# A three-stage attention and mixing kernel on one core: the order of TensorE's steps is written out, and the other engines' targets follow from it

## The chip, the core and the metric

The kernel runs on one core of one Trainium2 chip. The metric is the device time of one execution in microseconds (us). Before the change it is 635.29 us, the median of three runs (633.85 to 635.33). The execution that the profile recorded took 632.69 us.

## The reference

Three blocks follow each other for a batch of 4, 448 positions and a width of 768 (12 heads of 64):

```python
scores = np.where(mask, -1e9, scale * q @ k.T)
x = softmax(scores) @ v                       # 12 heads, joined to 768 columns
theta = x @ w_theta
y = w_tok_r @ (x * cos(theta)) + w_tok_i @ (x * sin(theta))
u = x + y
x = u + relu(u @ w_ch)
logits = x @ w_gate                           # top 2 of 4 experts, softmax over the two
for e in range(4):                            # each expert is causal attention with one head of 64
    out += weight[e] * (softmax(mask(x @ wq[e] @ (x @ wk[e]).T)) @ (x @ wv[e]) @ wo[e])
```

All of it is float32.

## The kernel before

The program doesn't emit its instructions as they are written. Each call of an engine (`pe`, `act`, `dve`, `pool`, `sp`) is recorded by `Plan.add` (L203) as a step with its dependencies, its tiles and a cost estimate, and `Plan.issue` (L327) then plays a clock forward over five engines and emits steps as they become ready. All real instructions are emitted from one line of a helper (L508 in the profile), so that the profile tells them apart by tile and not by line. On the chip each engine follows the order in which its instructions were emitted, and waits where a result or a buffer isn't there yet.

What orders the steps is a due time. `plan.due` is set by the code around a step from the numbers in `K` (L521): a start and a length for each stage. `rank` (L313) pulls the due times of producers ahead of their users. In `issue`, an engine takes the ready step with the earliest due time; for TensorE a step of another kind than the last one (`mode`, L197) gets `K["pen"]` added (L436), so that the kinds are not mixed without need. Some steps may go to one of several engines (`either`, L286): copies out of PSUM to ScalarE or VectorE, scalings to GpSimd or ScalarE, and so on; `issue` decides by who would be done first. Buffers of one tag (`unit` 6, `pa` 2, `ph` 2, `raw` 3, `zn` 3, the PSUM tags `tp` 6 and `mm` 2; L545 to L547) are handed out in the order in which the program's text asks for them (`turn`).

The stages, per batch b, as the list `ORDER` (L520) has them:

- `attn1` (a0 to a3, L771): six pairs of heads. A pair (`pair`, L644) has six score matmuls with 64 rows and one of 448 columns with 128 rows (tiles `tp<-raw`), softmax on VectorE and ScalarE into `pa`, scaling by GpSimd and ScalarE, then `pa` is transposed: either by 16 TensorE transposes (`tp<-ident,pa`) that are copied to `ph` by ScalarE or VectorE, or, for the pairs in `BYDVE`, on VectorE and by 16 DMAs `ph<-pa` from SyncE. 20 matmuls `tp<-ph,vt` end it.
- `mixing` (m0 to m3, L812): x is split into a high and a low part of the type fp32r (`hl`), since a matmul in fp32r is a single pass; three products each stand for one full product. Six theta products of 18 matmuls (`mm<-hl,unit`), sine and cosine into `zt`, transposes (`tp<-ident,zt`), copies and differences into `zn`, and six products of 21 matmuls (`mm<-wt,zn`).
- `project` (p0 to p3, L875): six products with w_ch and four for queries and keys (`mm<-zt,unit`, 18 matmuls each, the latter into `qp`), and the values and gate logits (`mm<-unit,zt`, 260 columns).
- `attn2` (c0 to c3, L980): two pairs as in `attn1` but from `qp`, and six products with wo (`tp<-hc,c`).

Weights are read once as float32, split on VectorE, ScalarE and GpSimd, and written to DRAM (`scr<-unit`); later batches load the split form (`unit<-scr`), two tiles for one product. All DMAs are issued by SyncE (SP), in one order. The kernel starts with 24 transposes of the identity (`mm<-ident`) before the first scores.

Of the kernel before, what the change touches and what calls it, by code (L numbers as in the profile page):

```python
# [23 lines left out]
P = 128  # L24
# [96 lines left out]
SWITCH = 200.0  # L121
MODE = SWITCH
# [4 lines left out]
class Step:  # L127
    __slots__ = ("calls", "soft", "heirs", "after", "options", "done", "engine", "cost", "due", "deps", "users", "waiting", "ready", "tiles", "fresh", "order", "lag", "pc", "lk", "issued", "at", "mode")


class Plan:
# [3 lines left out]
    def __init__(self, nc, tc):  # L135
        self.nc, self.tc = nc, tc
        self.steps = []
        self.due = 0.0
        self.after = 0.0
# [8 lines left out]
    def cost(self, engine, name, out, ins, kw):  # L148
        n = out.width if isinstance(out, View) else 0
        psum = any(v.root.psum for v in ins)  # L150
        if engine == "tensor":
# [5 lines left out]
            if self.mode(ins, name):  # L157
                return 8.0 + 0.86 * n
# [4 lines left out]
        if engine == "vector":  # L163
            if name == "tensor_tensor_reduce":
                n = ins[0].width
            if name == "tensor_reduce":
                n = ins[0].width
            if name == "transpose":
                return 66.0 + 1.13 * n
# [27 lines left out]
    def mode(ins, name):  # L197

        if name != "matmul" or ins[1].dtype != F32:
            return 0  # L200
        return 1 if ins[0].idx.shape[0] == 1 else 2 if ins[0].width == 64 else 0

    def add(self, engine, name, *args, **kw):  # L203
# [13 lines left out]
        else:  # L217
# [5 lines left out]
            step.due = self.due  # L223
            step.lag = 0.0
            step.mode = self.mode(ins, name) if engine == "tensor" else 0
            step.after = self.after
# [44 lines left out]

    def claim(self, view):
# [40 lines left out]
    def rank(self):  # L313
# [12 lines left out]

    def issue(self):  # L327
# [6 lines left out]
        self.rank()  # L334
# [56 lines left out]
        while count < len(self.steps):  # L391
# [13 lines left out]
            for e in order:  # L405
# [5 lines left out]
                for x in avail[e]:  # L411
# [4 lines left out]
                    if pick is not None and due >= best:  # L416
                        break
# [15 lines left out]
                    if e != "tensor":  # L433
                        pick = x
                        break
# [15 lines left out]
                if e == "tensor":  # L451
                    if now < COLD:
                        end += cost
                    if s.mode != mode:
                        end += SWITCH
# [55 lines left out]
class Engine:  # L511
# [3 lines left out]
    def __getattr__(self, method):  # L515
# [5 lines left out]
K = {"path": 0.9449731, "hop": 186.6965, "slack": 134.3007, "war": 624.4051, "ahold": 15406.4476,  # L521
# [9 lines left out]
     "warm": 24}  # L531
# [525 lines left out]
```

## Time and profile before

| | us |
|---|---|
| median of three runs | 635.29 |
| profiled execution | 632.69 |
| its span, from the first to the last instruction | 630.9 |
| TensorE busy with matmuls | 607.5 |
| VectorE busy | 424.1 |
| ScalarE busy | 327.0 |
| GpSimd busy | 119.8 |

The page first gives the busy time of each engine over the span. TensorE (PE) is the engine with the largest share, and its instructions are fixed in number, so that its idle time and its place in time are what to look at. Two queries tell those: the busy time by stretches of the span, and the waits of an engine, with what ended them. A stretch in which two engines are both nearly full needs a look at both.

### The profile page before, as it was taken

The numbers are of one execution on the slowest core, as the hardware profiler recorded it, in microseconds if no ns is written. First come the engines' busy times: TensorE is split into PE (matmuls) and PEld (weight loads), VectorE is DVE, ScalarE is ACT, GpSimd is POOL, SyncE is SP. The second block draws the span as 40 slices with busy tenths as digits, with TensorE's granted clock in tenths as the row PEclk, the third lists the DMA queues.
The fourth block names the chain that finished last, engine by engine and source line by source line (L and its number), as shares of the span: only waits on it lengthen the run. The fifth ranks groups of instructions, "written<-read, shape, count | busy, mean of one in ns | idle before, by whom it ended". The sixth has DMA issues, their size and how long they took to land.

```text
span 630.9 us, 12382 instructions
## 1 busy us (share of the span) xinstructions
PE 607.5 (96%) x4320; PEld 525.7 (83%) x4320; DVE 424.1 (67%) x1294; ACT 327.0 (52%) x869; POOL 119.8 (19%) x219
## 2 busy tenths in 40 slices
PE   7899989999998999999999999999999999999987
PEld 5686868789896999988878978988888999999876
DVE  4799999998847865347677688527756596515260
ACT  5999797553524643037767667126565251101473
POOL 3433356220112200004210213002110110000020
PEclk9899999999999999999999999999999999999999
DMA  9768541568749760685766771056753963157523
GB/s 332 273 218 284 171 173 29 162 218 297 245 130 277 232 229 2 196 244 146 243 187 208 267 255 31 1 147 196 226 150 112 314 183 102 32 181 238 161 62 122
DMA packets 54639, 114.76 MB, mean 182 GB/s; under 512 B 7601, under 2 KB 19377, under 8 KB 54577
## 3 DMA queue, kind: packets, MB, share of 16 engines
q1 hardware_dynamic: 54576, 113.98, 56.8%
q8 instruction: 34, 0.56, 0.4%
q14 instruction: 29, 0.23, 0.1%
HBM read 81.15 MB, written 21.26 MB: 162 GB/s over the span
## 4 chain that ended last, share of the span: by engine, by line
PE 70%; DVE 9%; DMA 3%; ACT 2%; SPq 1%; issue 1%; POOL 0%; DVEq 0%; ACTq 0%; POOLq 0%
PE mm L508 50%; PE tp L508 20%; DVE zt L508 3%; DMA unit<-scr 2%; DVE pa L508 2%; DVE cmb L508 2%; SPq L508 1%; ACT pa L508 1%; DVE st L508 1%; DVE tp L508 1%; DMA c<-scr 1%; DVE zn L508 1%; DMA vt<-v 0%; ACT L508 0%; POOL pa L508 0%
## 5 line engine op out<-in xcount | busy, mean ns | idle before, releaser
L508 PE MATMUL mm<-zt,unit 128*128 128x448 f32 x720 | 159.6, 373 | 0.6 <-ACT qp L508 0.6
L508 ACT ACTIVATE pa<-pa,st 128x128 f32<-128x128 f32 (+4 forms) x257 | 125.0, 516 | 44.5 <-DVE st L508 34.9
L508 PEld LDWEIGHTS mm<-zt,unit 128*128 128x128 f32 x720 | 133.9, 188 | 15.9 <-issue 4.0
L508 PE MATMUL mm<-wt,zn 128*128 128x448 f32 x504 | 117.3, 375 | 0.4 <-DVE st L508 0.4
L508 POOL TENSOR_SCALAR pa<-pa,st 128x384 f32<-128x384 f32 (+3 forms) x114 | 65.6, 588 | 222.7 <-DVE st L508 154.3
L508 PE MATMUL mm<-hl,unit 128*128 128x448 f32 x432 | 97.8, 376 | 3.9 <-DMA unit<-scr 2.0
L508 PEld LDWEIGHTS mm<-wt,zn 128*128 128x128 f32 x504 | 91.5, 188 | 9.6 <-issue 1.4
L508 PEld LDWEIGHTS mm<-hl,unit 128*128 128x128 f32 x432 | 79.7, 189 | 15.8 <-DVE zt L508 3.2
L508 DVE CUSTOM_DVE_ANT_0 pa<-tp,mask 128x384 f32<-128x384 f32 (+3 forms) x147 | 58.6, 444 | 10.6 <-PE tp L508 10.4
L508 PE MATMUL tp<-raw 64*128 64x384 f32 (+3 forms) x336 | 61.3, 425 | 0.0
L508 PE MATMUL tp<-ident,pa 128*128 128x128 f32 x336 | 45.3, 277 | 8.4 <-POOL pa L508 4.4
L508 ACT ACTIVATE pa<-tp,st 128x256 f32<-128x256 f32 (+3 forms) x77 | 37.7, 510 | 27.2 <-DVE st L508 27.1
L508 PEld LDWEIGHTS tp<-ident,pa 128*128 128x128 f32 x336 | 37.9, 141 | 15.9 <-POOL pa L508 7.4
L508 PEld LDWEIGHTS tp<-raw 64*128 64x128 f32 (+1 forms) x336 | 34.1, 190 | 16.9 <-issue 4.7
L508 ACT ACTIVATE ph<-tp 128x512 f32<-128x512 f32 x67 | 35.5, 593 | 22.5 <-PE tp L508 22.4
L508 PE MATMUL tp<-ph,vt 128*64 128x128 f32 (+1 forms) x960 | 46.6, 254 | 0.0
L508 PEld LDWEIGHTS tp<-ph,vt 128*64 128x64 f32 x960 | 42.3, 137 | 4.7 <-issue 2.8
L508 ACT ACTIVATE zn<-tp 128x384 fp32r<-128x384 f32 (+1 forms) x33 | 17.7, 541 | 48.7 <-PE tp L508 47.2
L508 DVE TENSOR_TENSOR zn<-tp,zn 128x512 fp32r<-128x512 f32 (+1 forms) x48 | 29.1, 618 | 17.8 <-ACT zn L508 17.6
L508 PE MATMUL mm<-unit,zt 128*128 128x260 f32 (+1 forms) x264 | 34.8, 289 | 1.2 <-DVE qp L508 1.2
L508 PEld LDWEIGHTS mm<-unit,zt 128*128 128x128 f32 (+1 forms) x264 | 32.6, 184 | 2.9 <-DVE qp L508 1.4
L508 DVE SCALAR_TENSOR_TENSOR xt<-mm,xt 128x448 f32<-128x448 f32 x24 | 15.0, 624 | 28.9 <-PE mm L508 28.6
(111 smaller groups left out, 781.6 us busy)
## 6 DMA issues: line engine op xcount, KB each, us to landing
unit<-scr SPq DMA_DIRECT2D x96, 384.0 KB, 4.2
scr<-unit SPq DMA_DIRECT2D x32, 384.0 KB, 3.5
raw<-qk SPq DMA_DIRECT2D x24, 480.0 KB, 4.7
ph<-pa SPq DMA_DIRECT2D x176, 64.0 KB, 2.0
c<-w SPq DMA_DIRECT2D x24, 384.0 KB, 3.7
vt<-v SPq DMA_DIRECT2D x24, 256.0 KB, 4.0
unit<-scr SPq DMA_DIRECT2D x18, 260.0 KB, 3.5
c<-scr SPq DMA_DIRECT2D x18, 256.0 KB, 4.0
```

The lines of the kernel that those rows point to most:

```text
L508: getattr(getattr(self.nc, engine), name)(*args, **kw)
```

## The change

TensorE's order is no longer found by due times. `K` keeps eight numbers, and a table `RUNS` lists blocks of TensorE's steps with a count: (b, n) means the next n steps of block b, where a block is the text between two calls of `plan.next()`. `line` puts the steps in this order and gives each a due time by adding up costs, among them a table `TURN` for the change from one kind of matmul to another. `issue` lets TensorE take the next step of that line and no other. `rank` then derives the rest: the turn of each tile among its tag by the time at which TensorE first needs it, a limit for a step from the tile that will need its buffer next, the due times of the other engines, and the earliest time of a DMA (`ahold` before its due time). Cost formulas of a few operations are changed slightly, and there are 16 transposes of the identity at the start where there were 24. The instructions of the stages, their shapes and the buffers stay.

```diff
-SWITCH = 200.0
-MODE = SWITCH
+TURN = [[0, 93, 93, 0, 0], [129, 129, 129, 130, 129], [-45, -15, -94, 7, -45], [-81, 94, 93, 0, 0], [0, 57, 57, 69, 0]]
...
+    def next(self):
+        self.place += 1
...
+    def line(self):
+
+        blocks = {}
+        for s in self.steps:
+            if s.engine == "tensor":
+                blocks.setdefault(s.place, []).append(s)
+        line = blocks.pop(-1, [])
+        for b, n in RUNS:
+            line += blocks.get(b, [])[:n]
+            blocks[b] = blocks.get(b, [])[n:]
+        for b in sorted(blocks):
+            line += blocks[b]
+        at, mode, last = 0.0, 0, {}
+        for s in line:
+            s.due = last[s.place] = at
+            at += s.cost + TURN[mode][s.mode] + (s.cost if at < COLD else 0.0)
+            mode = s.mode
+        return line, last
...
+                    if s.engine == "tensor":
+                        t.need = min(t.need, s.due)
+        for group in groups.values():
+            group.sort(key=lambda t: t.need)
+            for i, t in enumerate(group):
+                t.turn = i
+                if i + t.bufs < len(group):
+                    t.limit = group[i + t.bufs].need
         for s in reversed(self.steps):
-            if not s.users:
-                continue
-            path = s.lag if s.engine == "sync" else s.cost
-            latest = min(u.due for u in s.users) - path * K["path"] - K["hop"]
-            s.due = min(s.due, latest) if s.engine == "tensor" else latest
+            if s.engine != "tensor":
+                path = s.lag if s.engine == "sync" else s.cost
+                latest = min([u.due for u in s.users], default=last.get(s.place, 0.0) + 4000.0)
+                s.due = min([latest] + [t.limit - K["free"] for t in s.tiles if t.bufs]) - path * K["path"] - K["hop"]
+                if s.engine == "sync":
+                    s.after = max(0.0, s.due - K["ahold"])
...
-                    if pick is not None and due >= best:
-                        break
+                    if e == "tensor" and s is not line[place]:
+                        continue
...
-                    key = due + (K["pen"] if s.mode != mode else 0.0)
-                    if pick is None or key < best:
-                        pick, best = x, key
+                    pick = x
+                    break
...
-     "warm": 24}
+K = {"path": 2.8401784, "hop": 66.8344, "slack": -28.2445073, "war": 335.8402, "ahold": 36217.093, "free": -837.5953,
+    "warm": 16}
+RUNS = [(0,1), (1,1), (4,1), (2,16), (5,1), (8,1), (9,1), (6,16), (12,1), (13,1), (7,1), (3,1), (14,16), (10,16),
...
```

**VectorE (DVE) in the first pairs of heads of a0.** The rows are score and mask reductions (ISA, `pa<-tp`), the two small operations of a softmax sum (`st`), and copies of transposed probabilities out of PSUM (`ph<-tp`). Before:

```order
L508 TENSOR_SCALAR st_233<-st_208 128x2
L508 RECIPROCAL st_233<-st_233 128x2
L508 COPY ph_213<-tp_222 128x512
L508 COPY ph_213<-tp_242 128x512
L508 COPY ph_257<-tp_256 128x512
L508 TENSOR_SCALAR st_233<-st_208 128x5
```

Now:

```order
L551 COPY ph_184<-tp_183 128x512
L551 TENSOR_SCALAR st_208<-st_197 128x2
L551 RECIPROCAL st_208<-st_208 128x2
L551 COPY ph_184<-tp_193 128x512
L551 COPY ph_184<-tp_215 128x512
L551 COPY ph_184<-tp_223 128x512
L551 ISA pa_165,st_179<-tp_230,mask_9_87 128x448
```

All four copies of the first pair are on VectorE now, where before two were and ScalarE had the others. Counted over VectorE's order up to the second `zn` difference of m0's last product, such copies are 17 now and were 9. TensorE's order ahead of the matmul that reads it holds the same work in both: 108 `mm<-hl,unit` matmuls, 119 `mm<-wt,zn`, 9 times 20 `tp<-ph,vt`, 11 groups of six scores and 186 (now 187) transposes; the 448-column scores are 10 before and 11 now, the transposes of the identity 24 and 16.

**SyncE (SP) at the start of m1.** The rows are DMA issues: `unit<-scr` loads the theta weights for m1, into buffers that the values of p0 have just left; `ph<-pa` are the 16 small DMAs of a pair in `BYDVE`; `scr<-unit` and `c<-wo` are weights on their way through the conversion. Before:

```order
L508 DMA scr_2_452_2296<-unit_2284 256x1x260
L508 DMA ph_2300<-pa_2168 32x512 x16
L508 DMA c_461_2404<-wo 128x256
L508 DMA scr_3_462_2410<-unit_2311 256x1x260
L508 DMA unit_2415<-scr_0_78_366 128x768
L508 DMA unit_2420<-scr_1_111_511 128x768
```

Now:

```order
L551 DMA ph_2176<-pa_1963 32x512 x8
L551 DMA scr_0_458_2337<-unit_2239 256x1x260
L551 DMA scr_1_459_2342<-unit_2264 256x1x260
L551 DMA scr_2_460_2346<-unit_2302 256x1x260
L551 DMA scr_3_461_2350<-unit_2323 256x1x260
L551 DMA scr_4_464_2361<-unit_2334 256x1x260
L551 DMA raw_2368<-qk 128x960
L551 DMA scr_5_466_2373<-unit_2357 256x1x260
L551 DMA unit_2457<-scr_0_130_595 128x768
L551 DMA unit_2466<-scr_1_135_627 128x768
```

The small DMAs now stand eight issues ahead of the loads, not two.

## Rows read from the trace of the kernel before

**Rows 1.** The page: the span, and TensorE's busy time in it.
```profile
span 630.9 us, 12382 instructions
PE 607.5 (96%) x4320; PEld 525.7 (83%) x4320; DVE 424.1 (67%) x1294; ACT 327.0 (52%) x869; POOL 119.8 (19%) x219
```

**Rows 2.** Busy time of each engine in four stretches; the first line names the columns.
```profile
core 0: us, PE busy (x) PEld busy (x) DVE busy (x) ACT busy (x) POOL busy (x), PEclk, DMA share, GB/s
0.00:20.00 20.00, 16.18 (x128) 12.44 (x129) 10.46 (x51) 12.44 (x39) 7.44 (x26) 1.00 0.93 348
20.00:133.00 113.00, 104.73 (x821) 84.03 (x820) 111.09 (x326) 91.65 (x244) 45.43 (x61) 0.98 0.54 177
133.00:600.00 467.00, 462.22 (x3170) 408.34 (x3169) 290.62 (x864) 207.36 (x546) 63.15 (x125) 1.00 0.58 182
600.00:631.00 31.00, 24.39 (x208) 20.84 (x206) 11.95 (x56) 15.58 (x43) 3.81 (x8) 0.99 0.30 94
```

**Rows 3.** TensorE's waits, 0 to 133 us: total, times, longest.
```profile
PE mm L508 <- POOL ident masks.py:199: 2.5, 1, 2.5
PE tp L508 <- DVE zn L508: 2.4, 2, 1.3
```

**Rows 4.** TensorE's waits, 133 to 600 us.
```profile
PE mm L508 <- DMA unit<-scr: 2.0, 2, 1.6
PE mm L508 <- DVE qp L508: 1.2, 1, 1.2
```

**Rows 5.** TensorE's waits, 600 us to the end.
```profile
PE tp L508 <- POOL pa L508: 2.5, 1, 2.5
```

**Rows 6.** VectorE's timeline: m0's last product gets its second zn difference (start, duration).
```profile
132.38 0.56 DVE L508 TENSOR_TENSOR zn<-tp,zn 128x384 fp32r<-128x384 f32 x1
```

**Rows 7.** VectorE's waits, 0 to 133 us.
```profile
DVE st L508 <- ACT pa L508: 2.6, 3, 1.3
...
DVE ph L508 <- PE tp L508: 0.4, 2, 0.2
```

**Rows 8.** The chain that ended last, unbroken pieces: start, duration, engine, instructions.
```profile
135.78 10.98 PE mm L508 x54
...
414.55 3.70 PE tp L508 x80
...
419.06 1.75 PE tp L508 x16
...
421.62 2.45 PE tp L508 x14
...
465.17 0.21 PE mm L508
465.37 0.36 PE tp L508 x3
```

**Rows 9.** Costliest groups: copies to ph (busy, mean ns; idle before, ended by).
```profile
L508 ACT ACTIVATE ph<-tp 128x512 f32<-128x512 f32 x67 | 35.5, 593 | 22.5 <-PE tp L508 22.4
...
L508 DVE COPY ph<-tp 128x512 f32<-128x512 f32 x17 | 11.5, 685 | 3.0 <-PE tp L508 2.9
```

**Rows 10.** Timeline of the start: GpSimd's masks, TensorE's identity transposes, the first score reduction.
```profile
0.73 0.83 POOL L508 MEMSET mask<- 128x384 f32 x2 [0.29 <-POOLq L1047]
...
2.45 3.61 PE L508 MATMUL mm<-ident 128*128 128x128 f32 x16 [2.45 <-POOL ident masks.py:199]
...
7.59 0.56 DVE L508 CUSTOM_DVE_ANT_0 pa<-tp,mask 128x384 f32<-128x384 f32 x1 [5.15 <-PE tp L508]
```

**Rows 11.** Costliest groups: the most frequent matmul (busy, mean ns).
```profile
L508 PE MATMUL mm<-zt,unit 128*128 128x448 f32 x720 | 159.6, 373 | 0.6 <-ACT qp L508 0.6
```

**Rows 12.** SyncE's timeline ahead of m1.
```profile
178.78 10.35 SPq L508 DMA_DIRECT2D ph<-pa  x16
...
189.85 0.58 SPq L508 DMA_DIRECT2D scr<-unit  x1
190.53 3.30 SPq L508 DMA_DIRECT2D unit<-scr  x4
```

More of the change, by code (lines that the diff above doesn't have):

```diff
@@ L127 @@
 class Step:
-    __slots__ = ("calls", "soft", "heirs", "after", "options", "done", "engine", "cost", "due", "deps", "users", "waiting", "ready", "tiles", "fresh", "order", "lag", "pc", "lk", "issued", "at", "mode")
+    __slots__ = ("calls", "soft", "heirs", "after", "options", "done", "engine", "cost", "due", "deps", "users", "waiting", "ready", "tiles", "fresh", "order", "lag", "pc", "lk", "issued", "at", "mode", "reads", "place")
 class Plan:
@@ L137, in __init__ @@
         self.steps = []
-        self.due = 0.0
-        self.after = 0.0
+        self.place = -1
         self.pe_time = 0.0
@@ L222, in add @@
             step.order = len(self.steps)
-            step.due = self.due
+            step.due, step.place = 1e9, self.place
             step.lag = 0.0
             step.mode = self.mode(ins, name) if engine == "tensor" else 0
-            step.after = self.after
+            step.after = 0.0
+            step.reads = engine != "tensor" and any(v.root.psum for v in ins)
             step.lk = self.locks(engine, name, out, ins)
@@ L319, in rank @@
                 d.heirs.append(s)
-        for s in reversed(self.steps):
-            if not s.users:
-                continue
-            path = s.lag if s.engine == "sync" else s.cost
-            latest = min(u.due for u in s.users) - path * K["path"] - K["hop"]
-            s.due = min(s.due, latest) if s.engine == "tensor" else latest
+        tiles, groups = {}, {}
+        for s in self.steps:
+            for t in s.tiles:
+                if t.bufs:
+                    if id(t) not in tiles:
+                        tiles[id(t)] = t
+                        groups.setdefault(t.tag, []).append(t)
+                        t.need, t.limit = 1e9, 1e9
+                    if s.engine == "tensor":
[6 more added lines that the diff above has]
+                    t.limit = group[i + t.bufs].need
+        for s in reversed(self.steps):
+            if s.engine != "tensor":
[4 more added lines that the diff above has]
+                    s.after = max(0.0, s.due - K["ahold"])
+        for group in groups.values():
+            if any(t.need == 1e9 for t in group):
+                group.sort(key=lambda t: t.need if t.need < 1e9 else t.first.due)
+                for i, t in enumerate(group):
+                    t.turn = i
     def issue(self):
@@ L333, in issue @@
         wake = [0.0]
-        self.rank()
+        line, last = self.line()
+        self.rank(last)
+        place = 0
         def lag(e, d):
@@ L451, in issue @@
                 if e == "tensor":
+                    place += 1
                     if now < COLD:
                         end += cost
-                    if s.mode != mode:
-                        end += SWITCH
+                    end += TURN[mode][s.mode]
                     mode = s.mode
@@ L642, in dense_sparse_attention_kernel, with pair @@
     UNIT = [14, 10, 0, 6]
-    def pair(raw, vts, gate, dest, due, gap, by_dve):
-        plan.due = due
+    def pair(raw, vts, gate, dest, by_dve):
+        plan.next()
         raw = raw()
@@ L699, in pair @@
         norm(0, 2, [(part(j, 2), j) for j in range(2)])
[L700 removed]
+        plan.next()
         sc_ = pst("tp")
@@ L746, in moving @@
                 return pt[:, at:at + P]
-        plan.due = due + K["g3" if by_dve else "f3"] * gap
+        plan.next()
         o_ = pst("tp")
@@ L786, in attn1 @@
             x0[b, pr] = xp
-            pair(fetch, [vt[:, j] for j in range(2)], None, xp, due, gap, pr in BYDVE[f"a{b}"])
+            pair(fetch, [vt[:, j] for j in range(2)], None, xp, pr in BYDVE[f"a{b}"])
     def mm3(o, ws, rhs, nk):
@@ L848, in trans @@
         def trans(m):
-            tick()
+            plan.next()
             zns[m] = []
@@ L868, in mixing @@
                 trans(m + 1)
-            tick()
+            plan.next()
             zn = zns.pop(m)
@@ L900, in values @@
         def values():
-            tick()
+            plan.next()
             wv = load_unit(22, NVG)
@@ L906, in values @@
             for c in range(4):
-                tick()
+                plan.next()
                 w = CW[c]
@@ L983, in attn2 @@
         for r in range(2):
-            due = due0 + r * gap
-            hl.append(pair(lambda: qps[r], [v2[r][:, :, j] for j in range(2)], g7[:, r, :], None, due, gap, r in BYDVE[f"c{b}"]))
+            hl.append(pair(lambda: qps[r], [v2[r][:, :, j] for j in range(2)], g7[:, r, :], None, r in BYDVE[f"c{b}"]))
         for m in range(NK):
             wu = unit(100 + m, 2 * P, 1, "c1")[0].rearrange("p h (r j) -> p h r j", r=2)
-            plan.due = K[f"w{b}"] + m * K[f"lw{b}"]
+            plan.next()
             o = pst("tp")
@@ L1009, in dense_sparse_attention_kernel @@
         kind, b = what[0], int(what[1])
-        {"a": attn1, "m": mixing, "p": project, "c": attn2}[kind](b, K[what], K["l" + what])
+        {"a": attn1, "m": mixing, "p": project, "c": attn2}[kind](b)
     plan.issue()
```

60 lines of the change are left out of this document (20 added, 40 removed), and 34 rows, old and new, of tables (K, RUNS).

## The prediction

> **What bounds the kernel now.** I read the page first: TensorE is busy for 607.5 of 630.9 us and nothing else comes near it [rows 1]. But for eight transposes of the identity its instructions are the same before and after, so only three things can change the time: where it waits, what it does in vain, and what lies around it. The table of stretches says where it waits [rows 2]. In the first 20 us it idles 3.8 us, up to 133 us another 8.3, then in 467 us only 4.8, and after 600 us 6.6. So the kernel has a front, a long full middle, and a tail.
>
> In the front VectorE is the cause: from 20 to 133 us it is busy for 111.1 of 113 us, and TensorE's waits there are largely for VectorE's results, next to a first one for the identity [rows 2, 3]. In the middle the waits are few: seven that make up the 4.8 us, the longest two for a load of weights (2.0 us) and one for the bank that a `qp` copy holds (1.2) [rows 4]. In the tail 2.5 us are the gate of the last expert, which must be known before the last transposes [rows 5]; most of the rest comes after the last matmul.
>
> **The front, in numbers.** I take one place: the second `zn` tile of m0's last product, which VectorE ends at 132.9 us [rows 6]. VectorE has by then been busy 10.5 + 111.1 = 121.5 us and idle 11.4. TensorE's own work ahead of the matmul that reads it, from unbroken pieces of the chain [rows 8], is 227 fp32r matmuls at 10.98/54 = 0.203 (46.2 us), nine groups `tp<-ph,vt` at half of 3.70 (16.7), eleven score groups at 2.45 with their 448-column one, less 0.9 since one of those comes later (26.0), 186 transposes at 1.75/16 = 0.109 (20.3), and the identity transposes, 16 in 3.61 us and eight at the transposes' spacing (4.5) [rows 10]. Sum 113.7. TensorE is thus 19.2 us late there, and VectorE's 121.5 us of work and 11.4 of idling explain it: the front is a queue at VectorE.
>
> **What the change does to it.** Ahead of the same place VectorE has 17 copies to `ph` and had nine. At 685 ns [rows 9] the eight cost 5.4 us; the other rows ahead of it, counted and priced the same way from their groups, come out 0.5 us lower. So VectorE has 126.4 us to do. Nothing hides this, since VectorE is full and TensorE waits for it; it counts one for one.
>
> Against it stands idling. GpSimd makes the identity first now, not after the masks. The masks took 0.83 us for their two memsets and some 0.3 for a select [rows 10], and TensorE's first wait was for the identity [rows 3]. So the warm-up transposes start 1.1 us earlier, and with them the first scores and VectorE's first reduction, which waited 5.15 us [rows 10]. Bounds for this gain are 0 (if the first load is late) and 1.1; I take 1.1. Of VectorE's other idling, 4.6 us, the larger named part is waiting for ScalarE's sums [rows 7]. The new order gives VectorE reductions of a second and third pair to do meanwhile, so I take half, 2.3; the ends are 0 and what the slower rival needs. That makes 5.7 + 2.3 = 8.0 us idle (of 11.4), and VectorE is done at 134.4.
>
> One wait earlier binds still harder. The first `zn` tile of that product is done 1.1 us before the second, but TensorE has twelve matmuls (2.4 us) between the two. So TensorE passes the place at 134.4 + 1.3 = 135.7: the front costs **+2.8**. Ahead of it TensorE has done one 448-column score more than before, so behind it **-0.9**.
>
> The Trainium skill, page "Perfetto Trace Analysis", section "Optimizing Scalar/DVE Operations", says that where VectorE is saturated some of its work should go to ScalarE. This change sends eight copies the other way. The trace bears the rule out so far as VectorE is full in the front, ScalarE is not (91.7 of 113 us), and a copy costs 593 ns there against 685 [rows 2, 9]. What the rule would make of the time is the third rival below.
>
> **Switches between kinds of matmul.** The change prices these with a table. Counted over TensorE's order, the switches between products and transposes fall from 143 to 90, those around scores and `tp<-ph,vt` from 135 to 130. The first kind costs nothing that I can see: a lone fp32r matmul between transposes takes 0.21 us, and three transposes after it 0.36 [rows 8], hardly more than their spacings. The second is in the group prices already, which hold a group's entry and exit [rows 8]; five fewer of 135 are worth a small part of one group, by estimate -0.5 to +0.5. I take **0**.
>
> **The middle.** Seven waits make 4.8 us. Each costs more than it shows: a matmul's row is 373 ns long while starts are 203 apart [rows 8, 11], so that 0.17 us of every wait lies under the last matmul's end. With 7 x 0.17 = 1.2 the middle holds 6.0 us. What can be had of it I read at the longest wait. SyncE spent 10.35 us on sixteen small `ph<-pa` issues, then over 1 us on two others, and only then issued the loads for m1, at 190.53 [rows 12]. In the new order eight of the small issues, six writes and one load stand ahead, and the loads come out in one block right as the values release their buffers. The transfer itself stays, and what covers it (448-column scores and one group `tp<-ph,vt`) is about 4 us as before, without those two. I expect the two load waits gone, the `qp` and bank waits halved since blocks of 18 now stand whole, and a few new short ones: three quarters of 6.0, **-4.5**, ends 0 and -6.0 (and above 0 by what new waits may cost: the third and fourth rivals).
>
> **The tail.** The order still ends with values, the last pair's scores, wo products of c2 as cover, 32 transposes, two groups and 36 wo matmuls. Cover between the last value matmul and the first transpose is about 3.4 us in both (12 wo matmuls and a 448-column score), so the 2.5 us wait stays: **0**.
>
> **Sum**: 2.8 - 0.9 + 0 - 4.5 + 0 = -2.6. The profiled execution took 632.69 us, which gives 630.1; the median of the runs is 2.6 above that execution, so the forecast for the median is **632.7 us**, 0.4% faster.
>
> **The rivals.**
>
> 1. *The front runs without gaps and the middle without waits.* VectorE idles 2.0 us less and all 6.0 us of the middle go: -6.1, 629.2 us. For it: from 20 to 133 us VectorE idled only 1.9 us [rows 2]. It is a floor: with this order VectorE's work alone puts TensorE at the place no sooner.
> 2. *New waits in the middle.* TensorE takes the next step and no other, so one late tile holds it. If two thirds of the 6.0 us come back elsewhere, the sum is -0.1: 635.2 us, no change. For it: buffers are as many as before, and the loads still pass through one SyncE order.
> 3. *The front idles as now.* VectorE's idling stays at 11.4 less the start's 1.1, so that all added copies arrive at the end: 126.4 + 10.3 + 1.3 = 138.0, +5.1 for the front, sum -0.3: 635.0 us, no change. This is what the Trainium skill's rule named above would give here.
> 4. *VectorE stands behind its own copies: slower.* A copy to `ph` can't start before TensorE's four transposes, which wait for GpSimd's scaling; VectorE takes its rows in order, so reductions queue behind a copy that isn't ready, and ScalarE and TensorE behind those. Before, two of nine copies waited, 0.2 us each [rows 7]. If each of the 17 waits 0.4, VectorE idles 6.8 us more: +4.2, 639.5 us. It decides from 4.5 us more idling than I took, that is 12.5 us up to the place against 11.4 now. Against it: the copies stand behind a second pair's reductions in VectorE's order, so that a late copy has cover.
> 5. *The order that results is no other in effect*: same waits, 635 us. The counts above speak against it.
>
> **Chances.** Forecast 0.42; rivals 0.16, 0.12, 0.12, 0.15, 0.03. A difference of 0.3% (1.9 us) is about what a measurement can tell from no change. The first rival and four fifths of the forecast's case lie below that: 0.51 faster. The second, third and fifth rivals and the forecast's upper edge make 0.29 for no change. The fourth, and cases of the second and third with one wait more, make 0.20 slower. The range that leaves out 2 in 10 runs from 628.0, a little under the first rival, to 639.0, just under the fourth. The forecast's own range is 630 to 635.
>
> **What would show it.** In the new profile: the first score reduction at about 6.4 us; VectorE full to some 135 us and its idling before the last `zn` difference near 8 us; that difference ending at 134 to 135; TensorE's idle time in the middle near 1.5 us with no load of weights among its long waits; the last transposes still waiting some 2.5 us for the gate. The forecast is wrong if VectorE's idling in the front is over 12 us, if the middle's waits stay over 4 us, or if the tail's cover has shrunk.

## The result, and the profile after

The changed kernel takes **627.92 us** (median of four runs, 626.58 to 628.62) beside 634.57 us for the kernel before (633.04 to 635.33): a ratio of 0.9896, 95% interval 0.9867 to 0.9924. It is 1.0% faster, where the forecast was 0.4% (632.7 us, range 628.0 to 639.0): the measured time lies just below the range. Measured once more beside other runs (e13_again, below) it took 628.44 against 633.55 us, 0.9908 (0.9886 to 0.9930). Its profiled execution took 628.51 us with a span of 626.7, so the sum of the prediction's terms, forecast at -2.6 us, came out as 626.7 - 630.9 = -4.2.

The page of the changed kernel, the lines that answer to [rows 1]:

```profile
span 626.7 us, 12367 instructions
...
PE 608.1 (97%) x4312; PEld 528.4 (84%) x4312; DVE 419.7 (67%) x1282; ACT 329.5 (53%) x870; POOL 129.2 (21%) x232
```

TensorE's busy time over the whole span is the same within 0.6 us, and the span is 4.2 us shorter: on the whole it is idling that went. The same table of stretches as in [rows 2]:

```profile
0.00:20.00 20.00, 16.78 (x79) 11.69 (x80) 11.89 (x58) 11.88 (x37) 7.21 (x27) 0.91 0.64 228
20.00:133.00 113.00, 103.39 (x845) 84.19 (x846) 110.55 (x325) 90.83 (x243) 43.39 (x63) 0.98 0.59 195
133.00:600.00 467.00, 466.65 (x3213) 414.30 (x3212) 289.64 (x870) 214.12 (x562) 75.17 (x136) 1.00 0.60 181
600.00:627.00 27.00, 21.31 (x180) 18.24 (x179) 7.62 (x32) 12.67 (x30) 3.43 (x7) 1.00 0.41 126
```

Idle time by stretch is now 3.2, 9.6, 0.35 and 5.7 us, where it was 3.8, 8.3, 4.8 and 6.6. Of the three parts of the forecast the front got worse, as it said, and the middle gave up nearly everything. TensorE's waits in the changed kernel, the first three of 0 to 133 us, then all of 133 to 600 and of 600 to 627 us (to be held against [rows 3, 4, 5]):

```profile
PE tp L551 <- POOL pa L551: 5.1, 5, 2.0
PE mm L551 <- DVE zn L551: 2.0, 2, 1.4
PE tp L551 <- ACT pa L551: 1.5, 2, 0.9
...
PE mm L551 <- DVE hl L551: 0.4, 1, 0.4
...
PE tp L551 <- POOL pa L551: 1.4, 1, 1.4
PE tp L551 <- DMA c<-scr: 0.4, 1, 0.4
```

One wait is left of the middle's seven, and the gate's wait in the tail is 1.4 us instead of 2.5. The place at which the prediction closed its account of the front, in the timeline of the changed kernel (start, duration, engine, operation):

```profile
133.27 5.51 PE L551 MATMUL mm<-wt,zn 128*128 128x448 f32 x25
...
133.92 0.69 DVE L551 TENSOR_TENSOR zn<-tp,zn 128x512 fp32r<-128x512 f32 x1
...
135.05 0.55 DVE L551 TENSOR_TENSOR zn<-tp,zn 128x384 fp32r<-128x384 f32 x1
```

VectorE's last difference ends at 135.6 us (before 132.9, [rows 6]), and m0's last matmul, which takes the final 0.37 us of the first row, begins at 138.41. The same row of the kernel before puts it at 134.66:

```profile
130.93 4.10 PE L508 MATMUL mm<-wt,zn 128*128 128x448 f32 x19
```

From there to the end of the span it is 488.28 us, before 496.24. That gives the cleanest account of the change: **front +3.75, all that lies behind it -7.96**. All experiments below are read with these two numbers. The part behind the front, first of the kernel before and then of the changed one (columns as in [rows 2]):

```profile
134.66:630.90 496.24, 484.95 (x3366) 427.65 (x3364) 300.91 (x915) 222.19 (x586) 66.28 (x133) 1.00 0.56 176
138.41:626.70 488.29, 482.55 (x3363) 427.75 (x3361) 292.04 (x891) 224.30 (x587) 78.00 (x142) 1.00 0.58 178
```

TensorE idled there for 11.3 us and idles for 5.7, which is 5.55 of the 7.96 us; the other 2.4 us are busy time.

### The profile page after: what moved, and what is told of

Its sections match the earlier page's. It is cut to its first block, busy times and chain, and to the rows that moved or that the text cites. A ratio compares the mean times of both kernels' runs of the same rounds, so it can differ in the third digit from the quotient of the medians.

```text
span 626.7 us, 12367 instructions
## 1 busy us (share of the span) xinstructions
PE 608.1 (97%) x4312; PEld 528.4 (84%) x4312; DVE 419.7 (67%) x1282; ACT 329.5 (53%) x870; POOL 129.2 (21%) x232
## 4 chain that ended last, share of the span: by engine, by line
PE 83%; DVE 12%; DMA 2%; issue 1%; ACT 1%; POOL 1%; POOLq 0%; DVEq 0%; ACTq 0%
PE mm L551 54%; PE tp L551 28%; DVE pa L551 3%; DVE cmb L551 3%; DVE zt L551 2%; DMA vt<-v 1%; ACT pa L551 1%; DVE zn L551 1%; DVE st L551 1%; POOL pa L551 1%; DMA c<-scr 1%; DVE unit L551 0%; DVE xt L551 0%; DVE hl L551 0%; DVE sm L551 0%
## 5 line engine op out<-in xcount | busy, mean ns | idle before, releaser
L551 PE MATMUL mm<-zt,unit 128*128 128x448 f32 x720 | 152.8, 370 | 0.0
L551 ACT ACTIVATE pa<-pa,st 128x256 f32<-128x256 f32 (+4 forms) x251 | 121.0, 513 | 38.2 <-DVE st L551 36.0
L551 PE MATMUL mm<-wt,zn 128*128 128x448 f32 x504 | 111.2, 372 | 2.6 <-DVE zn L551 2.0
L551 POOL TENSOR_SCALAR pa<-pa,st 128x384 f32<-128x384 f32 (+4 forms) x120 | 67.1, 575 | 210.9 <-DVE st L551 176.5
L551 PEld LDWEIGHTS mm<-wt,zn 128*128 128x128 f32 x504 | 92.1, 188 | 12.7 <-DVE zn L551 3.7
L551 DVE CUSTOM_DVE_ANT_0 pa<-tp,mask 128x256 f32<-128x256 f32 (+3 forms) x147 | 58.7, 446 | 15.3 <-PE tp L551 14.7
L551 ACT ACTIVATE pa<-tp,st 128x384 f32<-128x384 f32 (+3 forms) x77 | 38.0, 506 | 35.0 <-DVE st L551 31.8
L551 ACT ACTIVATE ph<-tp 128x512 f32<-128x512 f32 x58 | 30.9, 599 | 22.9 <-PE tp L551 22.6
L551 DVE CUSTOM_DVE_ANT_0 tp<-tp,mask 128x384 f32<-128x384 f32 (+3 forms) x77 | 33.2, 475 | 7.4 <-PE tp L551 5.7
L551 ACT ACTIVATE zn<-tp 128x512 fp32r<-128x512 f32 (+1 forms) x36 | 18.8, 547 | 35.9 <-PE tp L551 35.9
L551 PE MATMUL tp<-hc,c 128*128 128x448 f32 x144 | 34.0, 377 | 0.4 <-DMA c<-scr 0.4
```

What stands on the lines that cost most here:

```text
L551: getattr(getattr(self.nc, engine), name)(*args, **kw)
```

## The experiments

The table gives each version's median with its ratio to the kernel before, run beside it (633.03 to 633.75 us; 634.57 beside the first measurement of the change), and from its profile the time at which m0's last matmul begins and what lies behind that, in us. The versions were not run beside the change itself, except e14 and e15; their ratios are what compares. The two columns on the right come from one profiled execution each, which need not be like the median: that of e9 took 635.75 us, the longest of twelve, and that of e11 631.85, one of the shortest.

| | median | ratio (95%) | m0's last matmul | behind it |
|---|---|---|---|---|
| before, profiled execution | | 1 | 134.66 | 496.24 |
| the change, profiled execution | 627.92 | 0.9896 (0.9867 to 0.9924) | 138.41 | 488.28 |
| e1_old_line | 655.51 | 1.0358 (1.0336 to 1.0380) | 137.51 | 516.05 |
| e2_old_front | 636.14 | 1.0046 (1.0030 to 1.0062) | 138.28 | 496.87 |
| e3_old_middle | 648.94 | 1.0248 (1.0228 to 1.0269) | 138.51 | 509.37 |
| e4_old_margins | 647.76 | 1.0234 (1.0207 to 1.0260) | 150.38 | 496.85 |
| e5_ahold | 640.28 | 1.0098 (1.0072 to 1.0125) | 149.43 | 489.21 |
| e6_lead | 655.52 | 1.0341 (1.0304 to 1.0378) | 151.15 | 502.13 |
| e7_copies_act | 629.96 | 0.9942 (0.9920 to 0.9964) | 141.02 | 488.21 |
| e8_start_old | 628.37 | 0.9915 (0.9893 to 0.9938) | 139.53 | 488.37 |
| e9_p0_old | 632.07 | 0.9986 (0.9967 to 1.0005) | 139.18 | 494.79 |
| e10_tail_old | 631.73 | 0.9972 (0.9955 to 0.9989) | 137.06 | 492.97 |
| e11_switch200 | 634.77 | 1.0007 (0.9990 to 1.0024) | 143.31 | 486.76 |
| e12_warm8 | 628.08 | 0.9926 (0.9909 to 0.9943) | 136.66 | 488.24 |
| e13_again | 628.44 | 0.9908 (0.9886 to 0.9930) | 136.60 | 488.49 |
| e14_late_copies | 633.44 | 1.0002 (0.9987 to 1.0017) | 144.83 | 488.51 |
| e15_writes_first | 632.65 | 0.9979 (0.9962 to 0.9997) | 138.79 | 492.75 |

### The order, or the targets that follow from it

The first question was which half of the change emptied the middle. For e1, e2 and e3 (and e9, e10) `RUNS` holds another order, given as runs of consecutive steps of the program's text (first step, count); all else is the change's:

```diff
-        for b, n in RUNS:
-            line += blocks.get(b, [])[:n]
...
+        steps = [s for s in self.steps if s.engine == "tensor" and s.place >= 0]
+        for a, n in RUNS:
+            line += steps[a:a + n]
```

**e1_old_line.**

> The changed kernel, but TensorE's written-out order is replaced by the order that TensorE had before (the 24 against 16 transposes of the identity apart). Turns of the buffers, due times of the other engines and margins are derived as in the change. Theory A (the new order of TensorE's steps took the waits out of the middle): the middle idles 4 to 5 us again, 632 to 635 us. Theory B (the derived targets and turns did it, whatever the order): the middle idles under 1.5 us; the front has 13 copies to ph on VectorE up to the place where the change has 17, so it is no later than in the change: 625 to 628 us.

**e2_old_front.**

> TensorE follows its order of before up to the last matmul of m0's last product, and the order of the change behind it; all else as in the change. 13 copies to ph on VectorE ahead of the second zn tile of m0's last product, against 17 now and 9 before. If the front's term holds (TensorE late by VectorE's work, 2.7 us later in the change than before): that zn tile 1.5 to 3 us earlier than in the change (132.5 to 134) and the whole 625 to 626.5 us. Rival C (the middle is full only because TensorE comes to it late, so that the loads are in time): what the front gives comes back as waits in the middle, 627.5 to 628.5 us.

**e3_old_middle.**

> TensorE follows the change up to the end of m0, then its order of before up to about 575 us, then the change's tail; targets are derived. Theory A (order): 3 to 5 us of idling in the middle, 631 to 633 us. Theory B (targets): under 1.5 us, 627.5 to 629 us.

All three came out slower than any theory had them. For e3, the two largest waits of TensorE from 133 us on:

```profile
PE tp L545 <- DVE c L545: 7.1, 1, 7.1
PE mm L545 <- DMA unit<-scr: 3.1, 3, 1.4
```

The loads' waits are back with the old order, as theory A had it, but a wait of 7.1 us for a split tile of weights is new, and neither kernel has it: the derived targets let VectorE come late there. In e1 and e2 one wait for `zt` took 8.3 us in the front, in e1 another for a weight tile 6.9 us in the middle. e2's front, meant to be lighter, ended no earlier than the change's; behind it, where e2 has the change's own order, one wait for a load took 3.6 us and the stretch 8.6 us more than in the change. So theory B falls, and A is too small.

**e4_old_margins.** The other way round: TensorE's order is the change's, and six of the seven numbers in `K` take the values of before. The rule that derives the targets stays the new one.

```diff
-K = {"path": 2.8401784, "hop": 66.8344, "slack": -28.2445073, "war": 335.8402, "ahold": 36217.093, "free": -837.5953,
+K = {"path": 0.9449731, "hop": 186.6965, "slack": 134.3007, "war": 624.4051, "ahold": 15406.4476, "free": 0.0,
```

> TensorE's new order kept, but the six margins from which the other engines' targets come are those of before (path 0.945 for 2.840, hop 187 for 67, slack 134 for -28, war 624 for 336, ahold 15406 for 36217, free 0 for -838): producers are asked for with less lead, and a load may be issued at most 15.4 us ahead of its due time. Theory A: the order carries it, 627 to 629 us. Theory B: loads and copies come late again, 2 to 5 us of waits in the middle with loads of weights among them, 630 to 633 us.

647.76 us, and no wait of TensorE for `unit<-scr`: neither theory. The front's end comes 12 us later, and behind it 8.6 us more pass. Two parts of it alone:

**e5_ahold** (`"ahold": 15406.4476`) and **e6_lead** (`"path": 0.9449731, "hop": 186.6965`).

> The changed kernel with one margin of before: a load may be issued at most 15.4 us ahead of its due time, where the change allows 36.2. If the early loads are what emptied the middle: waits of TensorE for unit<-scr of 2 to 4 us come back, 630 to 632 us. If the ranking of the other engines' work is what counts: 627 to 629 us.

> The changed kernel with two margins of before: each step ahead of a user is due 0.945 of its cost and 187 ns earlier than the user, where the change takes 2.84 of its cost and 67 ns. If the ranking of VectorE's and ScalarE's work is what cost e4_old_margins its 20 us: most of them come back, 640 to 648 us, with waits for zt, pa and zn. If the loads did: 627 to 630 us.

The longest wait of e5 up to 140 us, and the two longest behind:

```profile
PE mm L551 <- DVE zt L551: 10.6, 1, 10.6
...
PE tp L551 <- POOL pa L551: 1.4, 1, 1.4
PE mm L551 <- DMA unit<-scr: 0.6, 1, 0.6
```

and of e6 behind 140 us:

```profile
PE tp L551 <- DMA ph<-pa: 8.0, 2, 4.0
```

With loads held back to 15.4 us, the stretch behind m0 stays at 489.2 us: early loads are not what emptied the middle. Of the 12 us that e5 loses, 11 lie in the front, where one wait takes 10.6. A shorter lead (e6) costs in both places (front +12.7, behind it +13.9) and more than the ranking theory had it (640 to 648 us): TensorE waits twice 4 us for `ph<-pa` transfers, and 6.7 us for a `zt` in the front.

**e11_switch200.** `TURN` holds 200 ns for each change of kind, 0 on the diagonal and between fp32r products and 448-column scores.

> The changed kernel with the same order of TensorE, but the planner's clock prices each change between kinds of matmul at 200 ns where the change has the table TURN. Nothing on TensorE moves; due times of the other engines shift a little. If the derived targets must only be roughly right: 627 to 629 us. If they were fitted to this one clock: 2 to 20 us slower, with one or two long waits, in the front above all.

634.77 us, a loss of 6 to 7 us with not one step of TensorE moved. The profiled execution (631.85 us, with a mean granted clock of 0.995, the share of its full clock that TensorE was given) shows the part of it that lies in the front: m0's last matmul begins at 143.31 us, 4.9 later than in the change, with 18 copies on VectorE; behind it are 486.8 us. Eight of the other eleven executions had a lower granted clock (0.989 to 0.991) and took 633.3 to 635.4 us; where they lose more is not shown. So the front did not hold with targets from this other clock, while the middle did: in all versions that have the change's order in front of m0's end and behind it, with its leads (the change twice, e5, e7, e8, e11, e12, e14), the stretch behind is 486.8 to 489.2 us, with m0's end anywhere from 136.6 to 149.4. So the middle is not full only because TensorE comes late to it, the rival C of e2. e2 itself does not fit that list: its last matmul of m0 comes at 138.28 and its order behind is the change's, but it needs 496.87 us there. The middle needs the front's order too, and why is not shown.

### What the order does in the middle

**e9_p0_old** puts back the old order for one stretch, that of the prediction's longest wait.

> The changed kernel, but TensorE follows its order of before from the end of m0 to the last theta product of m1 (some 400 steps, about 138 to 197 us in the change); everything ahead of it and behind it is the change's order, and targets are derived. In that stretch the kernel before waited 3.1 us (a load 1.6 us, 0.6 for a qp copy, and others). Theory A, local (each stretch of the order carries its own waits): 2 to 4 us slower than the change, 630 to 632 us. Theory B (targets would have removed those waits with either order): 627.5 to 628.5 us. Theory C (order and targets fit only as a whole, a piece of another order upsets the rest): 635 us and more, with waits in later stretches too.

Local, as theory A had it, in time (632.07, at the edge of its range) and place: the load waits of TensorE are back in this stretch, and no later one has a new wait of any length. From 140 to 215 us:

```profile
PE mm L545 <- DMA unit<-scr: 3.5, 2, 2.0
PE mm L545 <- DVE qp L545: 0.5, 1, 0.5
PE mm L545 <- DVE st L545: 0.2, 1, 0.2
```

These are 4.2 of the 6.5 us that e9's profile needs more behind the front; another 0.7 lies under four matmuls by the forecast's reckoning. The rest is TensorE's clock, by estimate: from 208 to 212 us, behind the second of the load waits, the granted clock is 0.57 (third number from the end), where the change has 1.00 from 200 to 220; 4 x (1 - 0.57) = 1.7 us.

```profile
208.00:212.00 4.00, 4.00 (x16) 2.60 (x16) 1.64 (x3) 0.00 (x0) 0.00 (x0) 0.57 0.86 307
```

SyncE's timeline shows why the loads are late. The changed kernel:

```profile
168.00 4.95 SPq L551 DMA_DIRECT2D ph<-pa  x8
...
178.33 6.35 SPq L551 DMA_DIRECT2D ph<-pa  x8
184.73 3.29 SPq L551 DMA_DIRECT2D scr<-unit  x5
...
192.95 2.79 SPq L551 DMA_DIRECT2D unit<-scr  x6
```

and e9:

```profile
183.37 10.39 SPq L545 DMA_DIRECT2D ph<-pa  x16
193.86 2.23 SPq L545 DMA_DIRECT2D unit<-scr  x3
196.17 3.81 SPq L545 DMA_DIRECT2D scr<-unit  x3
...
200.74 9.27 SPq L545 DMA_DIRECT2D unit<-scr  x7
```

With the old order the sixteen small issues stand in one piece again, as in [rows 12], three writes behind them still hold `unit` buffers, and the second set of loads waits for those. **e15_writes_first** leaves e9's order and lets those writes go first:

```diff
+        for s in self.steps:
+            if s.engine == "sync" and 60 < s.place < 80 and any(t.tag.startswith("scr") for t in s.tiles):
+                s.due -= 20000.0
+                s.after = max(0.0, s.after - 20000.0)
```

> e9_p0_old with one thing more: SyncE issues the writes of split weights to DRAM as soon as they are ready, so that three of them, which hold unit buffers, no longer stand behind sixteen small ph<-pa issues. TensorE's order is that of e9_p0_old. If those sixteen issues were what made the loads late: the two load waits of 1.5 and 2.0 us go or shrink under 1 us in sum, 2.5 to 3.5 us faster than e9_p0_old (632.1): 628.5 to 629.5 us. If the order of TensorE's values alone sets when the buffers come free: both waits stay, 631.5 to 632.5 us.

```profile
PE tp L550 <- DMA ph<-pa: 2.1, 1, 2.1
PE mm L550 <- DVE qp L550: 0.5, 1, 0.5
```

Both load waits are gone, so SyncE's order made them. The transfers that were passed are late by 2.1 us themselves now: behind the front the profile is 2.0 us shorter than e9's, and the median is no better (632.65 against 632.07, with ratios whose intervals overlap). In this stretch of the old order SyncE's time to issue is what runs short. In the change the first eight `ph<-pa` issues start 15.4 us earlier than e9's sixteen, and SyncE stands idle for 3.6 us ahead of the loads (from 189.3 to 192.95); that the earlier start is why the new order wins here is the likely reading, and was not tested alone. The Trainium skill, page "DMA: Bandwidth & Descriptors", section "Issuing engines are not separate DMA queues", says that the sequencer's time to initiate a DMA is usually small relative to the DMA itself. In this trace one such issue takes 0.65 us (10.39/16), about a third of the 2.0 us that a `ph<-pa` takes from issue to landing (median in the changed kernel's page), and what stands behind sixteen of them waits for the sum.

### The tail

**e10_tail_old.**

> The changed kernel, but behind about 575 us TensorE follows its order of before. The wait for GpSimd's first scaled part was 2.5 us before and is 1.4 us in the change. If the order of the last values and of the wo products made it shorter: 2.5 us again, 628.7 to 629.5 us. If VectorE's order of the gate's small operations did: 1.4 us, 627.5 to 628.3 us.

The wait for the first scaled part (from ScalarE here) is 3.3 us, more than either forecast. But e10 differs from before in one thing that bears on it: one of the two wo products that stand behind the last values as cover is done already in the part that follows the change, so that six wo matmuls are left ahead of the wait, not twelve. The cover and the transposes that wait, in e10, in the kernel before, and the transposes in e1_old_line, which has the old order as a whole:

```profile
602.69 1.75 PE L545 MATMUL tp<-hc,c 128*128 128x448 f32 x6
607.77 6.39 PE L545 MATMUL tp<-ident,pa 128*128 128x128 f32 x32 [3.33 <-ACT pa L545]
```

```profile
605.92 2.94 PE L508 MATMUL tp<-hc,c 128*128 128x448 f32 x12
611.31 3.73 PE L508 MATMUL tp<-ident,pa 128*128 128x128 f32 x32 [2.46 <-POOL pa L508]
```

```profile
632.09 5.61 PE L545 MATMUL tp<-ident,pa 128*128 128x128 f32 x32 [2.13 <-ACT pa L545]
```

The six missing matmuls are 1.2 us (2.94 - 1.75), and 3.3 less that is the 2.1 us of e1. So the old order waits 2.5 us with the old targets and 2.1 with derived ones, and the new order with derived ones 1.4: by these single executions the larger part of the gain, some 0.7 us, is the order's. (Behind the front e10 needs 4.7 us more than the change: 1.9 of waiting, and 2.5 because the 32 transposes take 6.39 us and not 1.97 + 1.91; the granted clock is 0.50 from 608 to 612 us, behind the wait, and 1.00 in the change.) What shortens the wait is seen on VectorE. Before, in the timeline from the first of the gate's operations (`rk`) to the gated factor:

```profile
606.48 0.21 DVE L508 TENSOR_TENSOR rk<-lg 128x64 f32<-128x64 f32 x1
...
607.76 0.62 DVE L508 COPY cmb<-tp 128x448 f32<-128x448 f32 x1
...
610.34 0.16 DVE L508 TENSOR_TENSOR st<-st,gt 128x2 f32<-128x2 f32 x1
```

and in the changed kernel:

```profile
602.04 0.22 DVE L551 TENSOR_TENSOR rk<-lg 128x64 f32<-128x64 f32 x1
...
605.03 0.16 DVE L551 TENSOR_TENSOR st<-st,gt 128x2 f32<-128x2 f32 x1
...
605.25 0.62 DVE L551 COPY cmb<-tp 128x448 f32<-128x448 f32 x1
```

From the first `rk` to the factor it is 3.9 us before and 3.0 now, above all since the copy of a finished wo product stands behind the gate's operations instead of among them. In e10 and e1 it is 3.6.

### The front

**e7_copies_act** moves two copies of each pair of a0 to ScalarE, **e14_late_copies** all copies of the pairs at 67 to 87 us (there the condition is `plan.place in (44, 48, 52)`):

```diff
-                plan.copy(pt[:, 512 * i:512 * i + 512], tp)
+                plan.copy(pt[:, 512 * i:512 * i + 512], tp, "s" if plan.place < 24 and i % 2 == 0 else "sv")
```

> The changed kernel, but two of the four copies to ph of each pair of a0 may only go to ScalarE: 13 on VectorE ahead of m0's last differences in place of 17. Theory F (the front is a queue at VectorE, the added copies count one for one): 4 copies of 685 ns less, m0's last matmul 2 to 2.7 us earlier than in the change (138.4 us there), 625.3 to 626.5 us. Rival (the front idles as much more at ScalarE, or the order behind was fitted to a late front): no gain or a loss, 628 to 634 us.

> The changed kernel, but the copies to ph of the last three pairs ahead of m0's end (67 to 87 us) may only go to ScalarE: 12 on VectorE ahead of m0's last differences in place of 17. e7_copies_act moved four copies of the first pairs, where ScalarE is full from 10 us on, and the front came later. Theory F2 (behind some 45 us VectorE alone is full and every copy there counts one for one): 5 copies of 685 ns, 2.5 to 3.4 us faster, 624.5 to 626 us. Rival (ScalarE's copies come late for TensorE there too): 628 us and more.

Both lose. VectorE's work up to its last `zn` difference is 124.4 us in e7 and 124.7 in e14, with 13 and 12 copies, against 124.9 with 17 in the change: other steps fill the place, since the planner chooses the engines of the rest anew. VectorE's idling rises from 10.7 us to 13.9 and 17.2. Two of TensorE's waits up to 140 us in e14:

```profile
PE mm L551 <- DVE xt L551: 4.0, 1, 4.0
PE tp L551 <- ACT pa L551: 3.3, 2, 2.4
```

The wait for `xt` is new, and those for ScalarE's `pa` are longer (1.5 us in the change), so results of both engines come later than in the change. The Trainium skill, page "Perfetto Trace Analysis", section "Optimizing Scalar/DVE Operations", says that moving some work to ScalarE may make sense where VectorE is saturated. VectorE was busy for 110.6 of 113 us, and the two moves cost 2 and 5 us against the change (629.96 and 633.44 against 627.92 to 628.44). They gain nothing here, but they don't settle the rule either: VectorE's work as a whole did not fall.

**e8_start_old** and **e12_warm8** change the start; e8 gives the masks an earlier due time than the identity and sets `"warm": 24`, e12 sets `"warm": 8`.

> The changed kernel with the start of before: GpSimd makes the masks ahead of the identity, and there are 24 transposes of it. If an earlier start reaches the end of m0 through VectorE, as the forecast took it (1.1 us; the first reduction came only 0.4 us earlier): 628.3 to 629 us. If the front swallows it: 627.6 to 628.2 us.

> The changed kernel with 8 transposes of the identity in place of 16. The first load of raw lands some 3.5 us after its issue at 0.74 us, so that the first scores can begin near 4.3 us in place of 4.97. If the start reaches the end of m0 one for one, as e8_start_old showed: 0.5 us faster than the change, 627.0 to 627.6 us. Rival (with fewer transposes ahead of them the scores run at the lower granted clock for longer): no gain, or up to 1 us slower, 628 to 629 us.

**e13_again** is the change itself.

> The change itself once more, beside the same runs of the kernel before as the two below. Its profile shows how much of the front's end (138.4 us for m0's last matmul) is the granted clock of that one execution: with the clock full in the first 20 us 136.5 to 137.2 us is expected (e10_tail_old and e12_warm8, which have nearly the same front, had 137.1 and 136.7). Time 626.5 to 629 us.

In e8 all 24 transposes stand ahead of the first scores (before, eight stood behind them), so that VectorE's first reduction begins at 9.44 us; in the change it is 7.19, in e12 7.06, in e13 6.53. The time from there to m0's last matmul is 130.1 us in e8, 129.6 in e12 and 130.1 in e13, each with a granted clock of 1.00 in the first 20 us, and 131.2 in the change's profile, where it is 0.91. So in these profiles the start passes through VectorE to the front's end one for one, and the change's first profile has another 1.1 to 1.6 us, which goes with its lower clock. e13's row of m0's last matmuls, 1.81 us earlier than in the first profile:

```profile
131.46 5.51 PE L551 MATMUL mm<-wt,zn 128*128 128x448 f32 x25
```

In the medians neither start differs from the change: 628.37 and 628.08 against 627.92 and 628.44. e8's start 2.9 us later than e13's does not show there, and e12's gain of half a us was not found, so one for one is not shown beyond the profiled executions.

## Why the prediction fell short

- **What bounds the kernel, and the sign: right.** Waits of TensorE in a front, a full middle and a tail; the front loses, the rest gives more.
- **The front, +2.8: near, with parts that were off.** Measured +3.75 in the first profile and 136.60 - 134.66 = +1.94 in e13. VectorE's work was 124.9 us (forecast 126.4), its idling 10.7 (forecast 8.0; 9.0 in e13). TensorE's wait for the identity fell by 1.1 us, from 2.5 to 1.4, as taken, but the first reduction, forecast at 6.4, came at 7.19 and at 6.53. The errors in work and idling are of opposite sign, so that the sum is closer than its terms: that is partly luck. That each copy counts one for one was not confirmed: the two experiments that moved copies could not hold the rest still.
- **Behind the front, -0.9 - 4.5 = -5.4: too small.** Here the two profiles of the change agree: -7.96 and -7.75. TensorE's idle time fell by 5.55 us, where the forecast had three quarters of 4.8, that is 3.6. Its busy time fell by 2.4; the forecast's -0.9 for the 448-column score and 0.9 for ends of matmuls that come out from under waits would be 1.8. These two and the 0 for switches were not tested alone, and some 0.5 us stays unexplained.
- **The middle, "three quarters of 6.0, -4.5": the first step that failed, by its size.** Six of seven waits went, and nothing new came: from 133 to 600 us idle time fell by 4.8 - 0.35 = 4.45, and by the forecast's own reckoning six waits less uncover another 6 x 0.17 = 1.0. So about -5.5, the last part an estimate. The mechanism at the longest wait, SyncE's sixteen issues ahead of the loads, was right: e9 brings the waits back and e15 removes them.
- **The tail, "the 2.5 us wait stays: 0": the second.** The cover was counted and was the same; the length of the gate's own chain on VectorE was not looked at. It fell from 3.9 to 3.0 us, above all by a copy of 0.62 us, and the wait fell to 1.4: -1.1.
- **From the sum to the median, "the median of the runs is 2.6 above that execution": the third.** The 2.6 us came from a median of three runs. Against the same profiled execution (632.69 us) the medians of 4 to 29 runs are only 0.3 to 1.9 us higher (633.03 to 634.57), and the changed kernel's median lay 0.6 us below its first profile and 1.5 above its second. How the miss of 4.8 us divides is luck, then: with the first profile the sum missed by 1.6 us and this step by 3.2; with e13's (span 625.1) the sum is -5.8 and missed by 3.2, and this step by 1.1 of the 4.3 that remain against 628.44. In the kernel before, the spread goes with the clock: of 29 executions beside e9 to e12, 19 had a mean granted clock of 0.994 or 0.995 and ten 0.997 or more, with medians of the span of 632.2 and 630.3 us. The profiled one (630.9 us) had 0.997.
- **The rivals.** The first (middle without waits) held for the middle and not for the front. The second did not come. The third's idling did come, 10.7 us against its 10.3 in the first profile (9.0 in e13), but VectorE had less work than it assumed and the stretch behind the front gave more, so that its 635.0 us did not. The fourth is refuted: VectorE idles 10.7 us, under the 12.5 that it needed, and its waits for `tp` at copies sum to 2.5 us over five. The fear behind the second, that one late tile holds everything, shows where order and targets do not match: e1, e2, e3, e5 and e6 each have a single wait of 6.7 to 10.6 us in some place. e4, e11 and e14 lose by several waits of at most 4.0.
- **The signs that were named.** The middle's idling is 0.35 us (forecast 1.5) with no load among its waits; the last difference ends at 135.6 and in e13 at 133.8 (forecast 134 to 135); the gate's wait is 1.4 (forecast 2.5). None of the three signs of being wrong came, though the forecast was: all three looked for less gain than forecast, not for more.
- **Small slips in the working.** Eight copies at 685 ns are 5.5 us, not 5.4, and a first reduction 1.1 us earlier than 7.59 comes at 6.5, not 6.4. Between the small DMAs and the loads for m1 stand seven issues, as the prediction has it, not eight. None of this decides anything.

Three things stay open: what in VectorE's and ScalarE's orders makes the front lose 5 to 13 us when a target shifts a little (e4, e5, e6, e11); whether the old targets with the new order would have done as well, as they can't be separated from the old rule; and what the new turns of the buffers and the changed cost formulas give by themselves.

## What to carry to other kernels

An order written out for the bounding engine paid here only where the other engines' work was ranked for exactly that order: the old order under the new rule was 3.6% slower, the new order with the old margins 2.3%, and both together 1% faster. Look at what stands ahead of a late transfer in its queue before blaming the transfer, but expect that whatever is moved behind becomes late next, unless the work that asks for it can be asked for sooner. A difference between one profiled execution and a median of three runs should not be carried over to another kernel: it depends on which execution was profiled. And what a long wait can do to the granted clock behind it belongs to its price.

## What the runs showed that was not expected

A wait of TensorE can cost more than its length, since the granted clock may fall behind it to 0.50, the lower of its two levels; and of two executions of one program with the same wait, one may show that and the other not. In the change's first profile and then in e13, the ten transposes behind a wait of 1.14 us:

```profile
13.25 2.40 PE L551 MATMUL tp<-ident,pa 128*128 128x128 f32 x10 [1.14 <-POOL pa L551]
```

```profile
12.59 1.31 PE L551 MATMUL tp<-ident,pa 128*128 128x128 f32 x10 [1.14 <-POOL pa L551]
```

From 13 to 17 us the granted clock is 0.57 in the first and 1.00 in the second. The ten take 1.1 us longer at the lower clock. Of the 1.81 us between the two ends of m0, 0.66 are there at the first reduction already, where the granted clock is 1.00 in both; that part is not explained. Behind a wait of 2.0 us near 28 us the clock falls in both, but not in e12. Behind the gate's wait it stays at 1.00 in the kernel before (2.46 us, 32 transposes in 3.73) and falls to 0.50 in e1 (2.13 us, 5.61) and e10 (3.33 us, 6.39). What decides between the two is not shown.

The executions of e10 fit that: those with a mean clock of 0.996 or more took 629.05 to 629.12 us, those with 0.992 took 631.64 to 633.26, though only one of the latter was profiled. A difference under 2 us between two single profiles of this kernel says nothing before their clocks are compared.
